# Attention rows: the small constant on the row sums moves from VectorE to GpSimd

## The chip, the cores and the metric

The kernel runs on one core of a Trainium2 chip. Its time is the device time of one execution, in microseconds. The core has five engines, each with a queue of its own that it works through in order: TensorE (PE, with its weight loads as PEld), VectorE (DVE), ScalarE (ACT), GpSimd (POOL) and SyncE (SP), which issues the transfers here. Engines wait for one another through semaphores.

## The reference

Three stages follow one another: attention over hash buckets (2 batches, 8 heads, 768 rows, 64 columns), a feed-forward layer with a rational activation, and a mixture of 8 experts with a balanced gate. The change lies in the first:

```
mask = q_bucket[:, :, :, None] == k_bucket[:, :, None, :]
scores = scale * np.matmul(q, k.transpose(0, 1, 3, 2))
scores = np.where(mask, scores, -1000000000.0)
scores = scores - np.max(scores, axis=-1, keepdims=True)
attn = np.exp(scores)
attn = attn / (np.sum(attn, axis=-1, keepdims=True) + 1e-09)
return np.matmul(attn, v).astype(np.float32)
```

Everything is float32.

## The kernel before

The attention goes through its 16 heads one after the other, and through each in three groups (`gi`, 48 in all) of two row tiles of 128 rows. For a row tile, `scores` lets TensorE make 128 x 768 scores in PSUM, VectorE takes the row extreme and writes the tile `e` to SBUF (L282), and ScalarE takes the exponential in place and adds up the rows (L283). The two tiles' row sums of a group stand side by side in `rs`, 128 x 2. `norm` adds the constant 1e-9 to `rs` on VectorE (L287), takes the reciprocal on VectorE (L288), and multiplies both tiles `e` by it on GpSimd (L290, two instructions of 128 x 768). This last pair is called the rows' product below.

Two groups later `trans` transposes the scaled tiles on TensorE (L304) into PSUM; ScalarE copies the high part to `pth` and VectorE subtracts it for the low part `ptl` (L109). Three groups later `values` multiplies by the head's values `sv` on TensorE (L319) into `av`, which ScalarE (`avt`) and VectorE (`xp`, L330) bring together, and GpSimd splits the result into `xh` and `xl`.

Meanwhile GpSimd prepares a later head in `prep_head_a`: q, k and v are each split into a high part (L100, `pool_hi`) and a low part (L103, `pool_lo`, which subtracts the high part from the source), called sq, sk and sv. The low part needs its high part. TensorE transposes sq and sk (L245), and `prep_head_b` makes the hashes (L259, and L260 on VectorE). The first weights of the next stage are narrowed in the attention as well: ScalarE (L169), GpSimd (L170), VectorE (L180 to L183), GpSimd (L186), then ScalarE and GpSimd again for the two parts. The program states this from the group `NG - 13` on; in the queues much of it stands earlier, the first at 12 us.

The order of instructions in each engine's queue in the attention is not written by hand. The program states them in one order, and a planner puts them into queues ahead of the run, from their dependences, the program's order and its own idea of their durations. Within a queue that order is then fixed. In the two stages after the attention the queues of TensorE, ScalarE, VectorE and GpSimd are in the program's order. The first product there is L350.

The loop over the groups, shortened:

```
scores(it, 0)
(prep_head_a, prep_head_b)[g](i + 1)
trans(ti, 0)
values(vi)
scores(it, 1)
trans(ti, 1)
trans(ti, 2)
norm(it)
```

Of the kernel before, what the change touches and what calls it, by code (L numbers as in the profile page):

```python
# [21 lines left out]
ALU = mybir.AluOpType  # L22
# [13 lines left out]
def kernel(  # L36
# [16 lines left out]
    pe, act, dve, pool, sp = nc.tensor, nc.scalar, nc.vector, nc.gpsimd, nc.sync  # L53
# [230 lines left out]

    def norm(gi):
        e, rs = es[gi]
        dve.tensor_scalar(rs, rs, 1e-9, None, ALU.add)  # L287
        dve.reciprocal(rs, rs)  # L288
        for j in range(2):
            pool.tensor_scalar(e[j], e[j], rs[:, j:j + 1], 0.0, ALU.mult, ALU.add)  # L290
# [425 lines left out]
    for it in range(NG + VLAG):  # L716
# [38 lines left out]
        if it < NG:  # L755
            norm(it)
# [176 lines left out]
```

## Time and profile before

| | |
|---|---|
| median of 3 runs | 1625.94 us (1624.62 to 1626.88) |
| the profiled execution | 1626.08 us |
| its span | 1624.3 us, 22172 instructions |
| TensorE busy over the span | 1554.5 us (96%) |
| VectorE | 1231.2 us (76%) |
| ScalarE | 621.4 us (38%) |
| GpSimd | 930.0 us (57%) |
| 48 additions, L287 on VectorE | 15.3 us busy, 318 ns each |

The shares are means over three stages with different limits; the attention ends near 290 us. The span runs from the first to the last instruction, and 1.8 us of the execution's time lie outside it. TensorE's busy time counts pipelined matmuls with modelled ends. The chain of waits goes back from the last instruction, at each step to what released it or to the instruction before it on its engine.

### The profile page before, as it was taken

To read this page: it belongs to the slowest core of one execution; us is meant where nothing else is said; L and a number is where in the kernel's file an instruction comes from. 1 tells how busy PE (TensorE), PEld (TensorE's weight loads), DVE (VectorE), ACT (ScalarE), POOL (GpSimd) and SP (SyncE) were. 2 spreads that over 40 slices of the span, in tenths; PEclk is the share of its full clock that TensorE was granted. 3 is DMA by queue.
4 is the path that set the end of the run, shared out by engine and by line. 5 is a ranking of instruction groups with operands and counts; after the bars stand their busy time and mean duration, and the time that the engine had idled before them with its cause. 6 is when DMAs were issued, how large, how long until landed. Compare 5 with 4: busy or idle time off the path is not lost.

```text
span 1624.3 us, 22172 instructions
## 1 busy us (share of the span) xinstructions
PE 1554.5 (96%) x8091; PEld 1354.9 (83%) x8091; DVE 1231.2 (76%) x2112; ACT 621.4 (38%) x1167; POOL 930.0 (57%) x1165
## 2 busy tenths in 40 slices
PE   6999999899999969999999999999999999999999
PEld 4888888677666857888898988989888898888987
DVE  7999999788999982776667666766666766677675
ACT  4888788787777833111111111111111111111111
POOL 7777785677777874356545545534544553553450
PEclk8999999999999989999999999999999999999999
DMA  5322220011112000001101101100110110010002
GB/s 166 84 81 77 81 76 15 27 52 53 65 52 66 1 26 27 27 27 40 39 27 39 40 27 35 44 26 27 40 39 27 40 40 27 31 48 27 26 1 78
DMA packets 49404, 71.83 MB, mean 44 GB/s; under 512 B 4368, under 2 KB 35088, under 8 KB 49296
## 3 DMA queue, kind: packets, MB, share of 16 engines
q1 hardware_dynamic: 48432, 68.85, 13.8%
q8 instruction: 64, 1.05, 0.3%
q10 hardware_dynamic: 864, 1.57, 0.3%
q14 instruction: 44, 0.36, 0.1%
HBM read 59.79 MB, written 3.15 MB: 39 GB/s over the span
## 4 chain that ended last, share of the span: by engine, by line
PE 70%; DVE 15%; POOL 5%; ACT 4%; issue 3%; DMA 0%; POOLq 0%; DVEq 0%
PE accb L595 32%; PE prod L530 28%; PE av L319 3%; PE pt L304 2%; DVE tq L378 2%; DVE tu L380 2%; DVE tr L379 2%; PE acca L401 2%; POOL e L290 1%; PE h L350 1%; DVE e L282 1%; DVE bits L182 1%; DVE bits L180 1%; DVE ptl L109 1%; DVE tu L372 1%
## 5 line engine op out<-in xcount | busy, mean ns | idle before, releaser
L530 PE MATMUL prod<-xb,ww 128*128 128x384 f32 x2688 | 532.2, 336 | 1.1 <-DVE xb L109 0.5
L530 PEld LDWEIGHTS prod<-xb,ww 128*128 128x128 f32 x2688 | 478.3, 188 | 35.3 <-ACT xb L106 0.9
L595 PE MATMUL accb<-wb,gh 128*128 128x512 f32 x1536 | 477.4, 392 | 0.0
L550 ACT ACTIVATE gh<-c 128x384 fp32r<-128x384 f32 x256 | 134.5, 526 | 772.2 <-DVE c L555 772.2
L606 DVE SCALAR_TENSOR_TENSOR osum<-accb,gp,osum 128x512 f32<-128x512 f32 x336 | 251.9, 750 | 209.2 <-PE accb L595 206.1
L595 PEld LDWEIGHTS accb<-wb,gh 128*128 128x128 f32 x1536 | 282.8, 188 | 36.6
L595 PE MATMUL accb<-wb,gl 128*128 128x512 f32 x768 | 304.9, 397 | 0.0
L100 POOL TENSOR_SCALAR ww<-ra 128x256 fp32r<-128x256 f32 x128 | 52.2, 408 | 415.4 <-PE prod L530 415.2
L551 DVE SCALAR_TENSOR_TENSOR gl<-c,gh 128x384 fp32r<-128x384 f32 x256 | 197.2, 770 | 3.9 <-ACT gh L550 3.6
L595 PEld LDWEIGHTS accb<-wb,gl 128*128 128x128 f32 x768 | 143.9, 187 | 30.5
L350 PE MATMUL h<-xh,wa 128*128 128x512 f32 x384 | 127.6, 395 | 5.8 <-DVE tu L373 5.7
L401 PE MATMUL acca<-gh,wb 128*128 128x512 f32 x384 | 128.0, 394 | 5.0 <-DVE part L413 2.7
L555 DVE TENSOR_TENSOR c<-prod,u 128x384 f32<-128x384 f32 x192 | 105.9, 552 | 30.1 <-PE prod L530 30.1
L109 DVE TENSOR_TENSOR ptl<-pt,pth 128x512 fp32r<-128x512 f32 x144 | 94.3, 680 | 15.3 <-ACT pth L106 14.5
L290 POOL TENSOR_SCALAR e<-e,rs 128x768 f32<-128x768 f32 x96 | 90.1, 950 | 24.3 <-DVE rs L288 14.7
L103 POOL TENSOR_TENSOR ww<-ra,ww 128x256 fp32r<-128x256 f32 x128 | 95.5, 746 | 10.7
L350 PEld LDWEIGHTS h<-xh,wa 128*128 128x128 f32 x384 | 72.1, 188 | 27.4 <-DVE tu L373 10.3
L401 PEld LDWEIGHTS acca<-gh,wb 128*128 128x128 f32 x384 | 72.1, 188 | 25.8 <-DVE part L413 5.1
L283 ACT ACTIVATE e<-e,nm 128x768 f32<-128x768 f32 x96 | 89.8, 935 | 8.5 <-DVE e L282 7.7
L282 DVE TENSOR_SCALAR_CACHE_REDUCE e<-s 128x768 f32<-128x768 f32 x96 | 90.8, 947 | 2.0 <-PE s L275 1.7
L304 PE MATMUL pt<-idr,e 128*128 128x128 f32 x576 | 82.4, 278 | 9.1 <-DVE ptl L109 4.0
L103 POOL TENSOR_TENSOR wb<-rb,wb 128x512 fp32r<-128x512 f32 x64 | 83.8, 1309 | 5.3
(169 smaller groups left out, 2453.8 us busy)
## 6 DMA issues: line engine op xcount, KB each, us to landing
ra<-in_moe_w_dram SPq DMA_DIRECT2D x32, 512.0 KB
rb<-in_moe_w_dram SPq DMA_DIRECT2D x32, 512.0 KB
ra<-in_moe_w_in_dram SPq DMA_DIRECT2D x16, 512.0 KB
rb<-in_moe_w_out_dram SPq DMA_DIRECT2D x16, 512.0 KB
qkv<-in_q_dram SPq DMA_DIRECT2D x16, 192.0 KB
qkv<-in_k_dram SPq DMA_DIRECT2D x16, 192.0 KB
qkv<-in_v_dram SPq DMA_DIRECT2D x16, 192.0 KB
a<-a SPq DMA_DIRECT2D x16, 192.0 KB
```

Source lines behind the costliest of these rows:

```text
L103: pool.tensor_tensor(lo, src, hi.bitcast(F32), ALU.subtract)
L109: dve.tensor_tensor(lo, src, hi.bitcast(F32), ALU.subtract)
L282: dve.tensor_scalar(e[j], s[:, 0:S], BIG, None, ALU.min, ALU.min, accum_out=nm)
L290: pool.tensor_scalar(e[j], e[j], rs[:, j:j + 1], 0.0, ALU.mult, ALU.add)
L304: pe.transpose(pt[:, c, j * P:(j + 1) * P], e[j][:, cc * P:(cc + 1) * P], idf)
L350: pe.matmul(hps, lhsT=a[:, c], rhs=x[:, c], start=m == 0, stop=m == 3 * KC - 1)
L401: pe.matmul(o, lhsT=l[:, js], rhs=r, start=f == 0 and m == 0, stop=f == QF - 1 and m == 2)
L530: pe.matmul(o, lhsT=w[:, i, c], rhs=x[:, j, c], start=n == 0, stop=n == 5)
L550: act.activation(gh, c, AF.Relu)
L551: low.append(lambda: dve.scalar_tensor_tensor(gl, c, 0.0, gh.bitcast(F32), ALU.max, ALU.subtract))
L595: pe.matmul(o, lhsT=l[:, ts], rhs=r, start=f == 0 and m == 0, stop=f == 1 and m == 2)
L606: dve.scalar_tensor_tensor(d, o, gate["p"][:, n, e:e + 1], d, ALU.mult, ALU.add)
```

## The change

The constant is added by GpSimd, in place, with a second addition of 0.0 in the same instruction. The reciprocal stays on VectorE and the product on GpSimd. A group's sums so pass from ScalarE to GpSimd, to VectorE, and back to GpSimd.

```diff
     def norm(gi):
         e, rs = es[gi]
-        dve.tensor_scalar(rs, rs, 1e-9, None, ALU.add)
+        pool.tensor_scalar(rs, rs, 1e-9, 0.0, ALU.add, ALU.add)
         dve.reciprocal(rs, rs)
         for j in range(2):
             pool.tensor_scalar(e[j], e[j], rs[:, j:j + 1], 0.0, ALU.mult, ALU.add)
```

## Rows read from the trace of the kernel before

**Rows 1.** Busy time by stage: start:end, us, engines' busy us (instructions), clock, DMA.
```profile
50.00:290.00 240.00, 226.13 (x1669) 203.89 (x1668) 224.56 (x485) 194.97 (x412) 178.06 (x220) 1.00 0.24 65
```

**Rows 2.** Chain of waits, 20 to 295 us, shares by line.
```profile
by line: PE av L319 15.4%; PE pt L304 10.1%; POOL e L290 8.6%; issue 6.6%; DVE e L282 6.3%; DVE ptl L109 5.6%; PE s L274 4.1%; PE s L275 3.8%; ACT e L283 2.6%; PE hp L259 2.3%; POOL c L186 2.2%; ACT pth L106 2.1%; POOL sq L103 1.8%; DMA qkv
```

**Rows 3.** Timeline of GpSimd from 139.6 us: start us, us, line, what, count.
```profile
140.86 0.52 POOL L100 TENSOR_SCALAR sq<-qkv 128x384 fp32r<-128x384 f32 x1
...
142.44 0.69 POOL L100 TENSOR_SCALAR sk<-qkv 128x384 fp32r<-128x384 f32 x1
143.21 1.32 POOL L103 TENSOR_TENSOR sk<-qkv,sk 128x384 fp32r<-128x384 f32 x1
144.52 1.80 POOL L290 TENSOR_SCALAR e<-e,rs 128x768 f32<-128x768 f32 x2
```

**Rows 4.** Pieces of the chain of waits in the attention: start us, us, what.
```profile
35.01 0.07 DVE rs L287
...
123.76 0.94 DVE rs L287
...
140.68 0.24 DVE rs L287
...
141.86 0.90 DVE c L182
...
266.72 0.16 DVE rs L287
...
291.87 2.73 PE h L350 x12
```

**Rows 5.** VectorE's groups, 0 to 300 us: busy us, mean ns, idle before.
```profile
L287 DVE TENSOR_SCALAR rs<-rs 128x2 f32<-128x2 f32 x48 | 15.3, 318 | 1.5 <-ACT e L283 0.9
```

**Rows 6.** Instructions on the tile rs: duration ns min/median/max, first and last start.
```profile
L287 DVE TENSOR_SCALAR rs<-rs x48: 148/180/1023, 28.2 to 285.1; 128x2 f32<-128x2 f32 x48
L288 DVE RECIPROCAL rs<-rs x48: 144/154/167, 29.2 to 285.3; 128x2 f32<-128x2 f32 x48
```

**Rows 7.** Timeline of VectorE, 136 to 160 us.
```profile
141.71 0.15 DVE L288 RECIPROCAL rs<-rs 128x2 f32<-128x2 f32 x1
...
151.22 0.15 DVE L287 TENSOR_SCALAR rs<-rs 128x2 f32<-128x2 f32 x1
151.28 0.94 DVE L282 TENSOR_SCALAR_CACHE_REDUCE e<-s 128x768 f32<-128x768 f32 x1
...
156.16 1.00 DVE L287 TENSOR_SCALAR rs<-rs 128x2 f32<-128x2 f32 x1
157.07 0.94 DVE L282 TENSOR_SCALAR_CACHE_REDUCE e<-s 128x768 f32<-128x768 f32 x1
```

**Rows 8.** Timeline of GpSimd, 151 to 162 us.
```profile
152.18 0.51 POOL L100 TENSOR_SCALAR sv<-qkv 128x384 fp32r<-128x384 f32 x1 [3.37 <-PE av L319]
152.78 1.01 POOL L103 TENSOR_TENSOR sv<-qkv,sv 128x384 fp32r<-128x384 f32 x1
...
156.12 1.01 POOL L103 TENSOR_TENSOR sq<-qkv,sq 128x384 fp32r<-128x384 f32 x1
```

**Rows 9.** GpSimd's groups, 0 to 300 us: busy us, mean ns, idle before.
```profile
L100 POOL TENSOR_SCALAR xh<-xp 128x256 fp32r<-128x256 f32 x24 | 9.9, 411 | 12.7 <-DVE xp L330 12.7
...
L170 POOL TENSOR_SCALAR c<-c 128x512 f32<-128x512 f32 x8 | 5.1, 635 | 1.8 <-ACT c L169 1.3
...
L698 POOL IOTA row<- 128x1 int32 x1 | 0.1, 128 | 0.0
```

**Rows 10.** Timeline of ScalarE at 140 us.
```profile
139.94 0.18 ACT L283 ACTIVATION_READ_ACCUMULATOR e<-e,nm 128x1 f32 x1
```

**Rows 11.** Timeline of GpSimd at the attention's start.
```profile
12.03 0.51 POOL L100 TENSOR_SCALAR sk<-qkv 128x384 fp32r<-128x384 f32 x1
12.62 0.61 POOL L170 TENSOR_SCALAR c<-c 128x512 f32<-128x512 f32 x1
13.20 1.01 POOL L103 TENSOR_TENSOR sk<-qkv,sk 128x384 fp32r<-128x384 f32 x1
```

**Rows 12.** Who waited for whom, 20 to 290 us: us in total, times, longest.
```profile
POOL sv L100 <- PE av L319: 25.0, 13, 3.4
```

## The prediction

> **What bounds the kernel now.** I read the stages first. In the attention's steady part, 50 to 290 us, VectorE is busy for 224.56 of 240 us, TensorE for 226.13 (its ends are modelled, so this is no peak), GpSimd for 178.06 [rows 1]. So VectorE has about 6% of the stage left and GpSimd 26%: seen by shares alone, a small operation belongs on GpSimd. Behind the attention the order of all compute engines is written out by hand and starts from the attention's last results, so what the attention wins or loses should pass through to the end nearly whole.
>
> The second view is the chain of waits over the attention. It doesn't stay on one engine. Products of TensorE hold the largest shares, and the rows' product on GpSimd (L290) has 8.6% of 275 us, 23.7 us [rows 2]; at 1.8 us a pair [rows 3] that is 13 of the 48 pairs. The addition that the change moves (L287) lies on the chain in eleven short pieces, of which rows 4 show the first, the last and two between; they sum to 3.5 us, and three of them (0.94, 0.92 and 0.53) hold most of it.
>
> The third view is the group of the addition itself. For two numbers per partition it takes 318 ns in the mean, 15.3 us in 48 [rows 5], but its median is 180 and its longest is 1023 ns, while the reciprocal of the same two numbers, next to it, always takes 144 to 167 [rows 6]. The timeline tells why it is worth looking at: the one at 151.22 us takes 0.15 and the next instruction starts after 0.06, the one at 156.16 takes 1.00 and the next starts after 0.91 [rows 7]. In the second case GpSimd was in the low part of a split, from 156.12 to 157.13, a subtraction of two SBUF tensors [rows 8].
>
> **What is removed.** 48 additions leave VectorE's queue. Each overlaps its follower by 0.09 us (0.15 less 0.06, and 1.00 less 0.91) [rows 7], so the queue gets back 15.3 - 48 x 0.09 = 11.0 us at most. That is the bound if VectorE set the pace throughout. Along the chain that did set the end it is 3.5 us [rows 4]. I take 3.5: where the addition is off the chain, VectorE has another wait a moment later.
>
> The long ones are the wait for a port. Row against rule: the addition at 156.16 ended when GpSimd's split did, and the reciprocal never waits [rows 6, 7]. The Trainium skill, "SBUF — State Buffer", section "Who interferes with whom", says that VectorE's tensor_scalar in a two-port mode and a GpSimd instruction exclude each other for a whole instruction, whoever starts first; the trace agrees (0.15 us against 1.00). By that rule all that lies above the median of the reciprocal, an estimate of 48 x (0.318 - 0.154) = 7.9 us, is a stall that cannot happen on GpSimd, whose own queue is in order, and the change would be a gain; this is the first rival below.
>
> **What is added on GpSimd.** No row shows a tensor_scalar of two elements there. A lower bound is the iota of one element, 0.128 us; an upper one the 256 columns of the high part xh, 0.411 us. The same kind of operation with two constants takes 0.635 us at 512 columns, so a straight line through these two leaves 0.19 us at two columns [rows 9]. I take that: 9.1 us of busy time in 48, between 6 and 20. Where GpSimd has idle time this is hidden by it (62 of 240 us [rows 1]). Where the rows' product is on the chain it is not: 13 pairs x 0.19 = 2.5 us, up to 5.3 at the upper bound.
>
> **What is moved: a wait across engines.** Before, ScalarE's row sums released the addition on VectorE, then the reciprocal followed some instructions later in the same queue, then GpSimd's product. After, the reciprocal waits in VectorE's queue until GpSimd has done the addition, and GpSimd's queue is in order too. So what counts is which GpSimd instructions the planner puts ahead of the addition. Behind the waiting reciprocal stand the row maxima (L282), the low parts of the transposes (L109) and the weights' narrowing, and TensorE waits for these.
>
> The row sums of one pair are complete at 140.12 [rows 10]. GpSimd then runs a train of splits of a later head, sq high, sq low, sk high, sk low, from 140.86 to 144.53, and the product only at 144.52 [rows 3]. The reciprocal stood at 141.71 to 141.86 [rows 7]: the product could have run 2.7 us earlier. The train's three places for one more instruction are the gap behind sq high, the start of sk high and the gap behind it. The planner, which orders the queues ahead of the run, fills the short gap between a high part and its low part when it has something ready (at 12.62 us L170 stands between sk high and sk low [rows 11]), yet it did not put the product into the gap at 143.13. So in its account GpSimd's train is at least 143.13 - 141.86 = 1.3 us earlier against VectorE than on the chip. The same shift moves the sums from 140.12 to at least 141.4 on GpSimd's line: past the gap behind sq high, which ends at 141.38. The addition then stands at 142.44, at 143.13 or at 144.52, ends 0.19 later, and the reciprocal starts 0.9, 1.6 or 3.0 us later than its 141.71. The chain of waits runs over VectorE here, through the addition at 140.68 and L182 behind the reciprocal [rows 4], so the delay is not covered. I count six such places in the timeline, one in each two heads (products behind a split train at 76.1, 109.7, 144.5, 178.2, 212.2 and 244.4) and take 1.5 us, near the middle place: 9.0 us, with 5.4 and 18 as ends.
>
> At the other places I take nothing. Five trains look like that of 156 us: the sums come as sq low starts, the addition on VectorE is held for 1.0 us anyway, and a GpSimd addition in the gap behind sk high gives the reciprocal back at about the same time. With the last heads, where there is no train, GpSimd is idle when the sums come.
>
> **Sum.** -3.5 + 2.5 + 9.0 = +8.0 us on the profiled execution's own 1626.08 us, which lies within 0.01% of the median of 1625.94: 1634 us. Own range of this case: 1630 to 1643, from the ends of the wait.
>
> **Rivals.**
> *Faster.* The planner puts the addition into the first gap, and VectorE keeps what it saves. For it: the queue of VectorE is the fullest, and the rule above. Against: only 3.5 us of L287 lie on the chain. Price: between -3.5 + 2.5 = -1 and -11.0 + 2.5 = -8.5; the middle is 1621 us. It decides if fewer than one reciprocal per train waits over 0.5 us for GpSimd.
> *Nothing measurable.* The two terms on the chain cancel, -3.5 + 2.5, and the waits fall where VectorE would have waited for ScalarE's pth: 1625 us. For it: the stage leans on three engines in turn, so a microsecond on one is often idle time on the next.
> *Much slower.* The split of v (sv high) waits for TensorE's av 13 times [rows 12], in the place shown with GpSimd idle for 3.37 us before it [rows 8]. If the addition is queued behind sv high it inherits that wait, and the reciprocal stops VectorE for 0.51 + 0.19 = 0.7 us more, behind sv low for 0.51 + 1.01 + 0.19 = 1.7: 13 x 0.7 to 13 x 1.7 is 9 to 22 us, with the -1 of the chain 1634 to 1647, say 1641 us, and the trains' waits come on top where both happen. Against: GpSimd was idle when the sums came, so the planner would have to see them in the other order. It decides if the addition follows sv in most heads.
> *The planner orders the whole stage anew.* Its order depends on durations, and one instruction more on another engine can shift later ones. It has no price of its own; it widens all cases.
>
> **How the numbers follow.** About 0.2%, 3.3 us, is what a measurement of this kernel tells from no change. Chances: the likeliest, 1634, 0.42; much slower 0.08; faster 0.28; nothing 0.22. So slower 0.50, same 0.22, faster 0.28. The range takes in the faster rival's bound (1618) and reaches to 1646, which leaves out the top of the slower cases and a new order with a large effect.
>
> **What would show it.** Right: VectorE's reciprocal gets idle time with GpSimd as releaser, some 6 to 15 us in all, most of it behind split trains; the addition on GpSimd takes 0.15 to 0.25 us; VectorE's busy time falls by 11 to 15 us and the attention is still longer; TensorE's first product of the next stage starts near 300 and not at 291.87 us [rows 4]. Wrong: the addition stands ahead of the trains, the reciprocal waits for nothing, the next stage starts earlier. It would also be wrong if the addition on GpSimd cost 0.4 us or more, or if the order of the splits themselves changed.

## The result: 1645.3 us, 1.2% slower, and all of it in the attention

The changed kernel takes 1645.3 us (1644.96 to 1646.54) beside 1626.39 us for the kernel before on the same chip: a ratio of 1.0116, 95% interval 1.0104 to 1.0128, or 18.9 us more. The direction was forecast and the time lies inside the whole forecast range (up to 1646), but outside the range given for this case (1630 to 1643), and the loss is more than twice the forecast 8.0 us. The profiled execution has a span of 1643.8 us.

The stages first, as in [rows 1].

```profile
50.00:290.00 240.00, 213.16 (x1538) 190.68 (x1536) 198.33 (x405) 181.59 (x381) 181.42 (x251) 0.99 0.24 67
```

VectorE fell from 224.56 to 198.33 us in the same 240 us and TensorE from 226.13 to 213.16. No engine is fuller than before but GpSimd, by 3.4 us, and that one still has 24% left. So no engine became the bound: all of them wait more. The piece of the chain of waits that opens the next stage stood at 291.87 us [rows 4]:

```profile
311.15 2.73 PE h L350 x12
```

It is 19.3 us later, the whole loss. What the engines wait for, 20 to 310 us (us in total, times, longest):

```profile
POOL rs L287 <- ACT e L283: 42.2, 19, 4.6
DVE rs L288 <- POOL rs L287: 34.5, 34, 2.8
ACT e L283 <- DVE e L282: 24.0, 30, 2.1
...
POOL e L290 <- DVE rs L288: 8.1, 23, 0.8
...
DVE ptl L109 <- ACT pth L106: 6.1, 9, 1.1
```

The second line is the wait that the change makes: VectorE's reciprocal for GpSimd's addition. The third is what it hands on: ScalarE's exponential waits for the row extremes (L282) that stand behind the reciprocal. The first is GpSimd standing at the addition until ScalarE has the sums. The split of v, which waited 25.0 us for TensorE [rows 12], now waits 0.8 us, so GpSimd has exchanged one wait for another. The additions themselves, by the tile `rs` as in [rows 6]:

```profile
L287 POOL TENSOR_SCALAR rs<-rs x48: 222/223/542, 27.8 to 304.4; 128x2 f32<-128x2 f32 x48
L288 DVE RECIPROCAL rs<-rs x48: 145/166/168, 28.3 to 304.6; 128x2 f32<-128x2 f32 x48
```

One place in full, a split train like that of [rows 3]. ScalarE:

```profile
152.25 0.21 ACT L283 ACTIVATION_READ_ACCUMULATOR e<-e,nm 128x1 f32 x1
...
153.83 0.98 ACT L283 ACTIVATE e<-e,nm 128x768 f32<-128x768 f32 x1
154.66 0.25 ACT L283 ACTIVATION_READ_ACCUMULATOR e<-e,nm 128x1 f32 x1
...
156.79 0.94 ACT L283 ACTIVATE e<-e,nm 128x768 f32<-128x768 f32 x1 [1.49 <-DVE e L282]
```

The first line completes the group's row sums, at 152.46 us (152.25 + 0.21). GpSimd:

```profile
152.06 0.41 POOL L100 TENSOR_SCALAR xh<-xp 128x256 fp32r<-128x256 f32 x1
152.56 0.73 POOL L103 TENSOR_TENSOR xl<-xp,xh 128x256 fp32r<-128x256 f32 x1
153.26 0.51 POOL L100 TENSOR_SCALAR sq<-qkv 128x384 fp32r<-128x384 f32 x1
153.86 1.02 POOL L103 TENSOR_TENSOR sq<-qkv,sq 128x384 fp32r<-128x384 f32 x1
154.84 0.51 POOL L100 TENSOR_SCALAR sk<-qkv 128x384 fp32r<-128x384 f32 x1
155.43 0.22 POOL L287 TENSOR_SCALAR rs<-rs 128x2 f32<-128x2 f32 x1
155.74 0.99 POOL L103 TENSOR_TENSOR sk<-qkv,sk 128x384 fp32r<-128x384 f32 x1
156.72 2.22 POOL L290 TENSOR_SCALAR e<-e,rs 128x768 f32<-128x768 f32 x2
```

VectorE:

```profile
152.04 0.95 DVE L282 TENSOR_SCALAR_CACHE_REDUCE e<-s 128x768 f32<-128x768 f32 x1
152.91 0.08 DVE L282 DVE_READ_ACCUMULATOR e<-s 128x1 f32 x1
155.69 0.17 DVE L288 RECIPROCAL rs<-rs 128x2 f32<-128x2 f32 x1 [2.69 <-POOL rs L287]
155.79 0.96 DVE L282 TENSOR_SCALAR_CACHE_REDUCE e<-s 128x768 f32<-128x768 f32 x1
```

The addition has its data at 152.46 and starts at 155.43, in the gap behind sk high, because four instructions stand ahead of it in GpSimd's queue. VectorE is idle for 2.69 us in front of a reciprocal of 0.17 us, with the next row extreme (L282) behind it, and ScalarE then waits 1.49 us for that extreme. The product that needs the reciprocal starts only at 156.72, behind sk low.

### The profile page after: what moved, and what is told of

It reads as the page before. It is cut to its first block, busy times and chain, and to the rows that moved or that the text cites. A ratio compares the mean times of both kernels' runs of the same rounds, so it can differ in the third digit from the quotient of the medians.

```text
span 1643.8 us, 22197 instructions
## 1 busy us (share of the span) xinstructions
PE 1559.1 (95%) x8091; PEld 1357.5 (83%) x8091; DVE 1222.5 (74%) x2064; ACT 623.4 (38%) x1167; POOL 940.7 (57%) x1213
## 3 DMA queue, kind: packets, MB, share of 16 engines
q1 hardware_dynamic: 48432, 68.85, 13.6%
## 4 chain that ended last, share of the span: by engine, by line
PE 69%; DVE 16%; POOL 5%; issue 4%; ACT 4%; DMA 1%; SPq 0%; DVEq 0%; POOLq 0%; ACTq 0%
PE accb L595 32%; PE prod L530 28%; PE av L319 3%; PE pt L304 2%; DVE tq L378 2%; DVE tu L380 2%; DVE tr L379 2%; POOL e L290 2%; PE acca L401 1%; PE h L350 1%; DVE bits L182 1%; DVE e L282 1%; DVE bits L180 1%; DVE tu L372 1%; DVE part L413 1%
## 5 line engine op out<-in xcount | busy, mean ns | idle before, releaser
L282 DVE TENSOR_SCALAR_CACHE_REDUCE e<-s 128x768 f32<-128x768 f32 x96 | 90.7, 949 | 2.8 <-PE s L275 2.2
```

The source lines that it names most:

```text
L282: dve.tensor_scalar(e[j], s[:, 0:S], BIG, None, ALU.min, ALU.min, accum_out=nm)
```

## The experiments

The theory ahead of the runs: what costs is the reciprocal's wait, and its size is set by the place of the addition in GpSimd's queue (theory 1). Its rivals: the 48 additions themselves fill GpSimd where it is on the chain (theory 2), and the planner, given one instruction on another engine, orders all queues anew (theory 3). All kernels change `norm`, whose lines in the kernel before are

```
dve.tensor_scalar(rs, rs, 1e-9, None, ALU.add)
dve.reciprocal(rs, rs)
```

### The addition left out, put aside, on ScalarE, and twice

Without the constant. Each row's largest exponential is 1, so the sum is at least 1, and in float32 it is the same with and without it.

```diff
-        dve.tensor_scalar(rs, rs, 1e-9, None, ALU.add)
```

> The constant is left out; the row sums are 1 or more (the largest term of a row is exp(0)), so the sum in float32 is the same. No engine adds, nothing crosses. Theory 1 (VectorE's reciprocal waits in its queue for GpSimd's addition, and that is the loss): faster than before by 1 to 11 us, 1615 to 1625, VectorE's reciprocal waits for nobody. Theory 2 (the 11.4 us more on GpSimd and its own wait for the sums are the loss): the same as theory 1 here. Theory 3 (the loss is the planner's other order, whatever the wait): this order differs from that of before about as much as the changed kernel's does, so it can come out near 1645 too.

Measured: 1627.69 us beside 1626.49, ratio 1.0007 [0.9998, 1.0017]. That misses the 1615 to 1625 of theory 1. The planner gave this kernel an order of its own; the same kernel in before's order is faster than before (below).

GpSimd adds into a tile that nobody reads, and the reciprocal takes the sums without the constant (shortened: `ra` and `rr` are new tiles of 128 x 2):

```diff
-        dve.tensor_scalar(rs, rs, 1e-9, None, ALU.add)
-        dve.reciprocal(rs, rs)
+        pool.tensor_scalar(ra, rs, 1e-9, 0.0, ALU.add, ALU.add)
+        dve.reciprocal(rr, rs); rs = rr
```

> As no_add, but GpSimd still does the 48 additions, into a tile that nobody reads; the reciprocal reads the sums without the constant. The order of TensorE, ScalarE and VectorE is that of no_add, GpSimd's is too but for the 48 additions. Theory 1: within 5 us of no_add, since nobody waits for the additions. Theory 2: 15 to 20 us above no_add. Theory 3: equal to no_add.

Measured: 1629.8 us, ratio 1.0019 [1.0010, 1.0028]. In the traces its queues have the same order as those of the kernel without the addition, instruction for instruction, but for the 48 additions. So in this order the load costs 2.1 us, with an uncertainty as large, and the wait seemed to carry most of the 18.9. But it is not the order of the changed kernel.

ScalarE adds, in its own queue directly behind the sums (`tiny` is a new tile that VectorE fills once with 1e-9):

```diff
-        dve.tensor_scalar(rs, rs, 1e-9, None, ALU.add)
+        act.activation(rs, rs, AF.Identity, bias=tiny)
```

> The constant is added by ScalarE, behind the row sums in its own queue, and VectorE's reciprocal waits for ScalarE. Theory 1: the wait is short since ScalarE has no long trains of its own there: 1620 to 1632 us, the reciprocal's waits under 10 us in all. Theory 2: at or below before, GpSimd has nothing more to do. Theory 3: anything from 1615 to 1645.

Measured: 1626.58 us, ratio 1.0000 [0.9990, 1.0009]. A crossing of engines need not bring a long wait: VectorE waits for this addition 0.9 us in all, 3 times.

GpSimd adds twice, the second time 0.0, both ahead of the reciprocal:

```diff
-        dve.tensor_scalar(rs, rs, 1e-9, None, ALU.add)
+        pool.tensor_scalar(rs, rs, 1e-9, 0.0, ALU.add, ALU.add)
+        pool.tensor_scalar(rs, rs, 0.0, 0.0, ALU.add, ALU.add)
```

> The changed kernel with a second addition (of 0.0) on GpSimd behind the first, before the reciprocal. Theory 1: each of the waits is longer by one addition, 0.22 to 0.3 us, at some 34 places: 1648 to 1657 us. Theory 2: the load on GpSimd doubles: 1657 to 1666. Theory 3: no rule, either way by 20 us.

Measured: 1653.95 us, ratio 1.0164 [1.0144, 1.0184], 8.7 us over the changed kernel. The waits, 20 to 310 us:

```profile
DVE rs L289 <- POOL rs L288: 34.5, 30, 4.2
POOL rs L287 <- ACT e L283: 28.5, 16, 3.6
```

VectorE waits no longer in all than in the changed kernel, yet the time rises. A load that no wait of VectorE shows would explain it, but another order would too. In these four the planner was free. But for the pair without the addition and with the unread one, its order differs from kernel to kernel, which leaves theory 3 open in every other comparison.

### The same, with the queues' order held

In the next kernels the order of the five queues in the attention is prescribed: an order edge without a semaphore leads from each instruction to the next in a stored list, taken from another kernel's queues. "After's order" is that of the changed kernel. "Before's order" is that of the kernel before, less VectorE's additions. In the traces of these kernels the queues show the order that was given to them, instruction for instruction by line and tile. Neither of the two kernels was itself run with its order prescribed.

```diff
-    qkv_pool_stack.close()
+    fix_queues(nc, tc); qkv_pool_stack.close()
```

No addition, in before's order and in after's:

> No addition at all, all queues in the order of before less the 48 additions. It prices what VectorE's queue gets back with nothing else changed. By the prediction's term 3.5 us less than before, 1623; at most 11 us less, 1615; if VectorE's time is worth nothing here, 1626.

> No addition at all, all queues in the order of the changed kernel less its 48 additions. Against no_add_before_order (1623.1) it prices the planner's other order alone, against aside_after_order (1633.1) the 48 additions on GpSimd alone. Theory 1 in its strict form (the wait is all): 1623 to 1626. If the order costs what is left over (about 8 us) and the load 2: 1630 to 1632.

Measured: 1623.13 us in before's order (0.9977 [0.9967, 0.9988], beside 1626.54) and 1624.98 in after's (0.9992 [0.9982, 1.0001], beside 1626.46). The first is the fastest kernel of this study, ahead of both kernels. VectorE's addition was worth 3.4 us; after's order costs 1.9 us, which is within the uncertainty of that difference.

The unread addition on GpSimd (as put aside above) in after's order, and in before's order with the addition ahead of the first GpSimd instruction that had started after the sums were there ("early place"):

> The data flow of pool_aside (GpSimd adds into a tile that nobody reads, the reciprocal reads the sums without the constant), with all five queues in the attention put by hand into the order of the changed kernel. So it differs from the changed kernel in one thing: the reciprocal doesn't wait for GpSimd. Theory 1 (the wait): 1628 to 1634 us, near pool_aside. Theory 3 (the order): 1642 to 1648, as the changed kernel. A value between them shares the loss out.

> GpSimd adds into a tile that nobody reads, in the order of before, at the same places as in after_before_order. Against no_add_before_order it prices GpSimd's load in that order: 2 to 3 us by the prediction's term, so 1625 to 1626; against after_before_order (1631.1) it prices the wait there, 5 us. If the load were the larger part: 1629 to 1631.

Measured: 1633.07 us (1.0036 [1.0023, 1.0049]) and 1629.72 (1.0024 [1.0014, 1.0034]). 48 additions for which nobody waits cost 8.1 us in after's order and 6.6 in before's, where the prediction's term gave 2.5. The changed kernel, in the same order as the first of them, takes 1645.3: the reciprocal's wait is 12.2 us.

The changed kernel's data flow in three other orders: that of the planner for the unread addition, before's with the early places, and before's with each addition directly ahead of its product:

> The other way round: the changed kernel's data flow (the reciprocal waits for GpSimd's addition) in the order that the planner gave pool_aside. Theory 1: above pool_aside by 8 to 25 us, 1638 to 1655. Theory 3: as pool_aside, 1628 to 1632.

> The changed kernel's data flow in the order of before, with each addition put into GpSimd's queue ahead of the first GpSimd instruction that in the trace of before started after the sums were complete. Theory 1: the reciprocal's places in VectorE's queue stay where they were, 0.3 to 2 us behind the sums, so the waits shrink to a few us in all and the time is 1625 to 1633. Theory 2 (GpSimd's load and its wait for the sums): 1640 or more. Theory 3: 1625 to 1630, since it is the order of before.

> As after_before_order, but each addition stands directly ahead of its rows' product in GpSimd's queue. If the place of the addition in GpSimd's queue sets the wait, the reciprocal now waits behind the whole train of splits and the product behind the reciprocal: by the trace of before the product followed the sums by 2.4 to 5.5 us and the reciprocal by 1 to 4, so some 1.5 us at 30 places or more: 1645 to 1680 us. If the place doesn't matter: 1631.

Measured: 1654.4 us (1.0172 [1.0157, 1.0187]), 1631.12 (1.0025 [1.0015, 1.0036]) and 1651.6 (1.0159 [1.0144, 1.0175]). The last two are the same instructions on the same engines and differ only in the places of the additions in one queue (41 of the 48 moved). Their waits, the early places first:

```profile
POOL rs L287 <- ACT e L283: 19.8, 13, 3.1
...
DVE rs L288 <- POOL rs L287: 0.7, 2, 0.5
```

and the late places:

```profile
DVE rs L288 <- POOL rs L287: 52.2, 32, 2.5
...
POOL e L290 <- DVE rs L288: 22.4, 46, 1.8
...
POOL rs L287 <- ACT e L283: 7.2, 6, 2.3
```

VectorE's wait for GpSimd goes from 0.7 to 52.2 us and the time by 20.5 us. The product, too, now waits for a reciprocal that starts right before it (22.4 us). GpSimd's wait for the sums runs the other way, and where it is 19.8 us the kernel takes the least time of the three.

In three orders there is a kernel without the addition, one with the unread addition, and one whose reciprocal waits for it. The load is the second less the first, the wait's price the third less the second:

| order | load, us | wait's price, us | VectorE's idle time for the addition, us |
|---|---|---|---|
| before's, early places | 6.6 | 1.4 | 0.7 |
| after's | 8.1 | 12.2 | 34.5 |
| the planner's for no addition | 2.1 | 24.6 | 39.6 |

Idle time is from 20 to 310 us; each difference is uncertain by 2 to 3 us. The wait is not paid in full. With the unread addition in after's order, VectorE's low parts wait for ScalarE like this:

```profile
DVE ptl L109 <- ACT pth L106: 22.6, 17, 4.8
```

In the changed kernel, with the same order, that is 6.1. So 16.5 us of the 34.5 replace waits that VectorE had anyway, which is most of what the time of 12.2 leaves out. In before's order the change still costs 4.6 us with the early places: -3.4 + 6.6 + 1.4. So there the place takes away nearly all of the wait's price, but not the load.

ScalarE adds, in before's order:

> The constant is kept and added by ScalarE directly behind the row sums, all else in the order of before less VectorE's additions. VectorE gets its 3.4 us back (no_add_before_order), ScalarE has 48 more short instructions of some 0.2 us, of which a third may lie on the chain, since ScalarE's exponentials are waited for: 1622 to 1630 us, with 1625 likeliest. If a crossing between engines cost much by itself, wherever it goes: 1630 or more.

Measured: 1631.1 us (1.0030 [1.0019, 1.0041]), 8 us over no addition in the same order, with 0.5 us of wait on VectorE. It lies above the 1622 to 1630 that were expected and in the band named for a dear crossing. The traces show another place for the loss. The first product of the next stage, with no addition and with ScalarE's:

```profile
289.20 2.76 PE h L349 x12
```

```profile
290.33 2.78 PE h L350 x12
```

Of the 8.4 us between these two profiled executions only 1.1 arise in the attention. From there to the end of the span it is 1332.1 us without the addition and 1339.4 with it, though no addition stands there. It is 1337.9 in the free order of the same data flow, and 1331.4 to 1333.2 in the other kernels. TensorE's products of the last stage take longer, first without and then with ScalarE's addition:

```profile
L529 PE MATMUL prod<-xb,ww 128*128 128x384 f32 x2688 | 532.1, 336 | 1.1 <-DVE xb L109 0.6
```

```profile
L530 PE MATMUL prod<-xb,ww 128*128 128x384 f32 x2688 | 537.0, 339 | 1.1 <-DVE xb L109 0.5
```

Why is open; both ScalarE kernels also hold the tile `tiny`, and no run separates that. So neither total prices ScalarE's addition. Within the attention it cost 1.1 us in before's order.

### What the load is made of

8.1 us of load were left, for which the sum had 2.5. Either the additions' execution costs it, or GpSimd's standing at them: 33.4 us of idle time in front of the unread addition in after's order. So the addition reads a constant tile and waits for no sums:

```diff
-        pool.tensor_scalar(ra, rs, 1e-9, 0.0, ALU.add, ALU.add)
+        pool.tensor_scalar(ra, thr, 1e-9, 0.0, ALU.add, ALU.add)
```

> As aside_after_order, but GpSimd's 48 additions read a constant tile and not the row sums, so they wait for no sums; the reciprocal reads the sums without the small constant (left out of the computation). The five queues' order is after's. If the 8.1 us of load (1633.1 against 1625.0) is GpSimd standing in its queue until the sums are there, it goes: 1625 to 1628 us. If it is the additions' execution, 48 x 0.237 us, it stays: 1631 to 1634 us. In between: both.

> The same in before's order with the additions at the early places (aside_before_order gave 1629.7, no additions at all 1623.1, so the load is 6.6 us); the small constant is left out of the computation here too. If the load is GpSimd standing for the sums: 1623 to 1626 us. If it is the additions' execution: 1628 to 1631 us.

Measured: 1632.26 us (1.0040 [1.0027, 1.0053]) and 1628.74 (1.0016 [1.0007, 1.0026]), beside 1626.28. Of 8.1 us 7.3 stay, of 6.6 us 5.6; the differences of 0.8 and 1.0 us are within the uncertainty of two medians (2 to 3 us, from the intervals). So what the addition waits for hardly matters, and the load comes with its execution. The runs don't price 33.4 us of standing, though, for most of it stays and only moves to the next instruction. GpSimd in after's order, with the unread addition:

```profile
POOL ra L287 <- ACT e L283: 33.4, 19, 3.4
...
POOL e L292 <- DVE rr L289: 2.6, 7, 0.5
```

and with the constant one:

```profile
POOL e L292 <- DVE rr L289: 29.4, 16, 3.4
```

The product stands where the addition stood. With no addition at all it stands 38.5 us. The chain of waits of the first kernel shows how an addition of 0.22 us costs more than that ("issue" is time in which the engine waits for nothing that the profile shows):

```profile
185.58 0.66 POOL sk L100
186.24 0.05 issue
...
186.31 0.85 POOL ra L287
187.16 0.07 issue
187.23 1.01 POOL sk L103
188.25 1.78 POOL e L292 x2
190.02 0.08 issue
190.10 0.22 POOL ra L287
190.33 0.08 issue
190.41 1.05 POOL c L186
```

The addition lies in 14 pieces on that chain, 4.43 us in all, so 0.32 us each, with an issue of 0.07 to 0.08 us behind each of the two shown; if every piece has one, 14 x 0.08 = 1.1 us, this makes 5.5 of the 7.3. In other orders the same count fails: the constant addition in before's order has 10 pieces of 2.3 us for a load of 5.6, and the unread one in the planner's order 16 pieces of 4.0 us for a load of 2.1. The one at 186.31 is stretched to 0.85. VectorE then ran:

```profile
186.05 0.42 DVE L332 TENSOR_TENSOR xp<-av,avt 64x256 f32<-64x256 f32 x1 [0.19 <-ACT avt L106]
186.39 0.68 DVE L183 SCALAR_TENSOR_TENSOR rb<-rb,c 128x512 f32<-128x512 uint32 x1
186.99 0.15 DVE L289 RECIPROCAL rr<-rs 128x2 f32<-128x2 f32 x1
```

The addition ends at 187.15, 0.08 us after L183's end at 187.07. All six additions of this kernel that take more than 0.25 us end 0.08 us after an end of one of VectorE's narrowing instructions (L180 to L183). That looks like the mirror image of the addition of 1.00 us on VectorE [rows 7, 8]. The Trainium skill, "SBUF — State Buffer", section "Who interferes with whom", says that a VectorE instruction with two SBUF inputs contends with a GpSimd instruction that reads SBUF; the trace agrees here (0.85 us against 0.22), though no run isolates it.

The last one keeps the changed kernel's data flow and order, but moves 24 of the 48 additions forward in GpSimd's queue, ahead of the first GpSimd instruction that, in the trace with the unread addition, had started after their sums:

> The kernel after in its own order, but 24 of the 48 additions stand earlier in GpSimd's queue, ahead of the first GpSimd instruction that started after their sums in the trace of aside_after_order; all is computed. If the place in GpSimd's queue sets the reciprocal's wait, most of its 12.2 us goes: 1631 to 1636 us, with VectorE's waits for GpSimd's addition well under 34.5 us. If the crossing from GpSimd to VectorE itself costs it: 1643 to 1646 us.

Measured: 1638.52 us (1.0075 [1.0060, 1.0090]), 6.8 us less than the changed kernel and 5.4 above the unread addition in that order. Its waits:

```profile
POOL rs L287 <- ACT e L283: 36.7, 25, 3.4
...
DVE rs L288 <- POOL rs L287: 11.1, 26, 0.9
```

VectorE's wait fell from 34.5 to 11.1 us and 6.8 of the 12.2 us that it cost came back. The place sets the wait in this order too; the time stays 2.5 us above the band that was expected, and the rest of the wait is in 26 short pieces.

## Why the prediction was wrong in size

The 18.9 us taken apart along after's order, each term a difference of two medians:

| term | forecast | measured | from |
|---|---|---|---|
| VectorE's addition gone | -3.5 | -3.4 | 1623.13 - 1626.54 |
| the planner's new order | none | +1.9 | 1624.98 - 1623.13 |
| 48 additions on GpSimd, nobody waits | +2.5 | +8.1 | 1633.07 - 1624.98 |
| the reciprocal waits for them | +9.0 | +12.2 | 1645.3 - 1633.07 |
| sum | +8.0 | +18.8 | measured at once: 18.9 |

The split belongs to this order: in another the load is 2.1 or 6.6 us and the wait 24.6 or 1.4.

**What is removed: right.** The eleven short pieces of the chain [rows 4] gave 3.5 us, the run 3.4. The bound of 11.0 us and the 7.9 us that the port rule promised were not to be had in these orders, and "a stall that cannot happen on GpSimd" was wrong too: there the addition was stretched to as much as 0.85 us. The rival "faster" falls with it, and not only because of the waits: even with no addition on any engine the kernel gains 3.4 us in these orders at most. "Nothing measurable" falls as well: in before's and after's order the load alone outweighs the gain.

**The load on GpSimd: the step that failed most.** The failed step is "Where the rows' product is on the chain it is not: 13 pairs x 0.19 = 2.5 us, up to 5.3". The duration was nearly right (0.223 us, between the bounds) and the count too (14 pieces on the chain of the kernel whose additions wait for nothing). What it left out is the stretched additions (0.32 us in the mean on the chain) and the issue behind each. Of the 7.3 us, 1.8 stay without a row. And a count of pieces on one chain, before's or another, is no price: measured loads run from 2.1 to 8.1 us, and not in step with the pieces. That it was near the 2.1 of one order is luck. What sets the load in an order stays open.

**The wait: mechanism right, size too small.** At the six trains VectorE's idle time in front of the reciprocal is 2.79, 2.14, 2.69, 2.69, 1.63 and 1.62 us, 13.6 in all, where I took 1.5 each. The place of the addition was as forecast: behind sk high, the middle place, in four of them, behind sq low in two. What failed is the reciprocal's own turn. In the kernel before it came 1.6 us behind the sums (141.71 against 140.12 [rows 7, 10]), with the addition and a row extreme between. In the changed kernel VectorE is free for it 0.5 us behind them (152.99 against 152.46), and 0.4 to 0.9 us at the six. So the same place makes it wait longer. And "At the other places I take nothing" was wrong: the other 28 waits add 20.9 us, most of it behind sq low, behind the earlier group's product and behind the narrowing of the weights (L186). That the 34.5 us cost only 12.2 is the other half: 16.5 us of VectorE's waits for ScalarE's pth went away in exchange. The sum's 9.0 us, near the 12.2, comes of two errors against each other: too little idle time, and all of it counted in full.

**The new order** had no price in the sum and cost 1.9 us, about the uncertainty of that difference. It matters in another way: the load of 2.1 us holds in the planner's order for no addition; taken over to the changed kernel it would put the wait at 15.5 us, where after's own order gives 12.2.

**"Much slower" behind sv** did not happen: sv waits 0.8 us for TensorE, and the late time has other places. Of what was to be seen, the reciprocal's idle time is 34.5 us where 6 to 15 were named, the addition on GpSimd is in its band, the next stage starts 11 us later than "near 300", and VectorE's busy time over the span fell by 8.7 us (1231.2 to 1222.5), less than the 11 to 15.

**Open:** what sets the load in each order (1.8 us of it without a row in after's), and why TensorE's products behind the attention take longer in the ScalarE kernels. The kernels with the unread and the constant addition also write the reciprocal to a tile of its own, which no run separates. The granted clock of TensorE differs too: from 120 to 150 us it was 1.00 before, but 0.89 with the unread and with the constant addition in after's order and 0.94 with none (means over stretches at full and at half clock), so a part of these differences of a few microseconds may be clock. It hardly explains the 7.3 us: in the three stretches of 30 us from 60 to 150 us the clock was 1.00, 1.00 and 0.89 with the constant addition and 0.94, 1.00 and 0.94 with none, the same in the mean.

## What to carry to other kernels

A small instruction moved to another in-order queue costs by its place there: price the wait from the instruction that the queue would already be running when the data comes, at every one of its occurrences, not only at the worst ones, and take off the waits that it replaces. An engine that is idle for a quarter of a stage is not free for a 0.2 us instruction: here 48 of them cost 2.1, 6.6 and 8.1 us in three orders with nobody waiting. Where a planner sets the order, compare only kernels with the same order, and look first for leaving the instruction out: without the constant, in before's order, the kernel takes 1623.1 us.

## What the hardware showed that was not expected

- GpSimd's addition of 128 x 2 numbers takes 0.222 us at the least and 0.223 in the median, and up to 0.85 beside VectorE's work.
- 34.5 us of VectorE's idle time for GpSimd cost 12.2 us in one order, 39.6 us cost 24.6 in another. In the first, 16.5 us of another wait went away for it.
- 33.4 us of GpSimd's idle time in front of an unread addition did not go when the addition no longer waited: 29.4 us then stood in front of the next instruction.
- One data flow on the same engines took 1631.1, 1638.5, 1645.3, 1651.6 and 1654.4 us in five orders, a spread of 23.3 us.
